# Strassen's seven products for the second layer of a fused attention and MoE kernel

## The chip, the cores and the metric

One core of one Trainium2 chip. The metric is device time in microseconds of one launch, as the median of several runs. The core has a matrix engine (PE in the profile, with PEld for its weight loads), a vector engine (DVE), an activation engine (ACT), GpSimd (POOL) and a queue engine for transfers (SP). They run beside each other and wait for each other by semaphores. PE writes its sums to PSUM banks, DVE and ACT read them from there.

## The reference

```python
# x (8, 8, 512, 64), state (8, 8, 32, 64): two small attentions per batch and head
attn_out = concat([softmax(x @ state.T / 8) @ state,
                   softmax(state @ x.T / 8) @ x], axis=2)   # (8, 8, 544, 64)
x = attn_out.transpose(0, 2, 1, 3).reshape(4352, 512)
h = x @ w_in                    # 512 -> 2048
r = maximum(h, 0)
g = s * (r * r) + b
out = g @ w_out                 # 2048 -> 512, float32
```

With the given inputs the term `b * sum(w_out)` makes up nearly the whole output: its root mean square is 0.0520, that of all the rest 0.0003 (worked out from the reference). The comparison of results therefore sees little of the product that the change is about.

## The kernel before

All matmuls are in fp16. A stage handles one batch: in sixteen steps (`f`) it computes the first layer of batch `s` (`mm1_x`, two matmuls of 512 columns into the tensor `h`), squares the result, and in between does one quarter of a 128-token block of the second layer of the batch before (`unit`, four matmuls of 512 columns into `o`). Pieces of the next batch's attention are put between the steps.

```python
def mm1_close(key, hps, ntok, f):              # after the two matmuls of a step
    ...
    nc.scalar.activation(r16[:, f % 2], hps, AF.Relu)          # ACT, 0.60 us
    if f % 2 == 1:
        gt = gpool.tile([P, 2, ntok], FP16, name=f"g_{key}_{f}", tag="g")
        nc.vector.tensor_mul(gt, r16, r16)                     # DVE, 0.69 us
        ...

def mm2_part(key, rr, f0, f1):                 # "unit": out[128 tokens] += g @ w_out
    ...
    for f in range(f0, f1):
        mm(ops, G[key, f][:, P * rr : P * rr + P], wof(f),
           start=(f == 0), stop=(f == NKF - 1))                # N = 512
    if f1 == NKF:
        ... evac(ops, ...)                     # DVE: out = s * psum + bias, then a DMA

# pieces of a stage s (cut)
at(0, lambda: att_stT(nb))
at(3, lambda: att_T(nb, [0, 1]))
at(3, lambda: att_M(nb, 0, "dve"))             # PSUM eviction on DVE, 1.2 us
...
for s in range(1, B):
    todo_s = pieces(s)
    for f in range(NKF):
        mm1_x(s, f)
        for fn in todo_s.get(f, []):
            fn()
        ...
        unit(todo.pop(0))
```

The softmax here doesn't subtract the row's maximum and nothing guards it: scores larger than these inputs give would overflow.

## Time and profile before

| | time, us | span of the profile, us | PE busy | DVE busy, us | ACT busy, us | POOL busy, us |
|---|---|---|---|---|---|---|
| before, given profile | 225.86 | 560.8 | 99% | 115.3 | 125.8 | 38.1 |
| before, profiled again in the experiments | 225.95 | 224.0 | 96% | 114.6 | 121.8 | 37.9 |

The given profile was slow: its execution lasted 560.8 us where the timed ones last 225.9. Its records show a granted clock of 1.000, so what slowed it is not shown. Lines from the page of that profile: the span, the engine totals, and two groups of instructions (line, engine, operation, what it writes and reads, shapes, count; then busy time and mean ns of one; then idle time before them and what ended it).

```profile
span 560.8 us, 3971 instructions
PE 555.9 (99%) x1628; PEld 169.0 (30%) x1628; DVE 115.3 (21%) x193; ACT 125.8 (22%) x211; POOL 38.1 (7%) x72
...
L64 PE MATMUL o<-wo,g 128*128 128x512 f16 (+1 forms) x528 | 329.7, 808 | 0.0
...
L314 DVE TENSOR_TENSOR g<-r 128x1024 f16<-128x1024 f16 x64 | 44.2, 691 | 142.0 <-ACT r L311 141.9
```

Two lines of its timeline (start, length, what, count). Thirty-two matmuls of N=512 follow each other from 528.50 to 547.55, which is 0.595 us each, and then 32 of N=256.

```profile
528.50 19.35 PE L64 MATMUL o_sr<-wo,g_sr 128*128 128x512 f16 x32
...
547.55 9.83 PE L64 MATMUL o<-wo,g 128*128 128x256 f16 x32
```

The mean of 808 ns is longer than the spacing of 595 ns: the records of neighbouring matmuls overlap.

### The profile page before, as it was taken

The numbers are of one execution on the slowest core, as the hardware profiler recorded it, in microseconds if no ns is written. First come the engines' busy times: TensorE is split into PE (matmuls) and PEld (weight loads), VectorE is DVE, ScalarE is ACT, GpSimd is POOL, SyncE is SP. The second block draws the span as 40 slices with busy tenths as digits, with TensorE's granted clock in tenths as the row PEclk, the third lists the DMA queues.
The fourth block names the chain that finished last, engine by engine and source line by source line (L and its number), as shares of the span: only waits on it lengthen the run. The fifth ranks groups of instructions, "written<-read, shape, count | busy, mean of one in ns | idle before, by whom it ended". The sixth has DMA issues, their size and how long they took to land.

```text
span 560.8 us, 3971 instructions
## 1 busy us (share of the span) xinstructions
PE 555.9 (99%) x1628; PEld 169.0 (30%) x1628; DVE 115.3 (21%) x193; ACT 125.8 (22%) x211; POOL 38.1 (7%) x72
## 2 busy tenths in 40 slices
PE   9999999999999999999999999999999999999997
PEld 3132222232233222332223223232223233334324
DVE  1442231212221212112211221112211111111101
ACT  3442122313221232113221232113221111111100
POOL 7010000100000001000010000000000000000011
DMA  9995000400060033004030120001000000000001
GB/s 202 205 132 87 1 37 9 86 19 19 1 112 20 19 75 57 19 19 76 0 56 19 39 57 20 19 19 39 11 7 19 20 19 19 19 20 19 19 19 39
DMA packets 38774, 23.69 MB, mean 42 GB/s; under 512 B 24100, under 2 KB 36644, under 8 KB 38756
## 3 DMA queue, kind: packets, MB, share of 16 engines
q0 software_dynamic: 15792, 16.72, 14.4%
q1 hardware_dynamic: 22548, 6.62, 5.8%
q8 instruction: 13, 0.21, 0.2%
q10 hardware_dynamic: 416, 0.10, 0.1%
q14 instruction: 5, 0.04, 0.0%
HBM read 17.33 MB, written 8.91 MB: 47 GB/s over the span
## 4 chain that ended last, share of the span: by engine, by line
PE 99%; DVE 0%; issue 0%
PE o L64 54%; PE h L64 27%; PE o_sr L64 3%; PE h_sr L64 3%; PE Mps L64 3%; PE warm_ps L64 2%; PE D L64 2%; PE xTps L64 1%; PE T L64 1%; PE V L64 1%; PE wsum_ps L64 0%; PE stTps L64 0%; PE bias_ps L64 0%; PE srT L64 0%; DVE M L251 0%
## 5 line engine op out<-in xcount | busy, mean ns | idle before, releaser
L64 PE MATMUL o<-wo,g 128*128 128x512 f16 (+1 forms) x528 | 329.7, 808 | 0.0
L64 PE MATMUL h<-a,M 128*128 128x512 f16 x256 | 180.2, 831 | 0.0
L311 ACT ACTIVATE r<-h 128x512 f16<-128x512 f32 x126 | 75.1, 597 | 335.9 <-PE h L64 335.9
L64 PEld LDWEIGHTS <-g 128*128 128x128 f16 x528 | 85.3, 166 | 189.5 <-issue 179.5
L64 PEld LDWEIGHTS <-M 128*128 128x128 f16 x256 | 44.4, 175 | 103.2 <-issue 102.7
L314 DVE TENSOR_TENSOR g<-r 128x1024 f16<-128x1024 f16 x64 | 44.2, 691 | 142.0 <-ACT r L311 141.9
L357 DVE SCALAR_TENSOR_TENSOR osb<-o,s_bc,bias_bc 128x512 f32<-128x512 f32 (+1 forms) x33 | 24.1, 734 | 126.5 <-PE o L64 126.5
L359 POOL DMA_DIRECT2D out_dram<-osb x31 | 16.9, 546 | 466.2 <-DVE osb L357 450.2
L256 DVE CAST M<-Mps 128x1024 f16<-128x1024 f32 x15 | 18.4, 1225 | 38.5 <-PE Mps L64 38.5
L64 PE MATMUL Mps<-wi,stT 64*32 64x512 f16 x256 | 22.8, 669 | 0.0
L64 PE MATMUL h_sr<-srdT,wi 128*128 128x256 f16 x64 | 22.6, 542 | 0.0
L64 PE MATMUL o_sr<-wo,g_sr 128*128 128x512 f16 x32 | 19.4, 836 | 0.0
L64 PEld LDWEIGHTS <-wi 128*128 128x128 f16 x64 | 11.3, 176 | 15.9 <-issue 11.9
L254 ACT CAST M<-Mps 128x1024 f16<-128x1024 f32 x13 | 13.2, 1012 | 6.4 <-PE Mps L64 6.3
L64 PEld LDWEIGHTS <-stT 64*32 64x32 f16 x384 | 5.0, 94 | 30.4 <-issue 27.9
L311 ACT ACTIVATE r_sr<-h_sr 128x256 f16<-128x256 f32 x16 | 6.1, 384 | 35.8 <-PE h_sr L64 35.8
L64 PE MATMUL warm_ps<-warm 128*128 128x512 f16 x16 | 10.0, 801 | 1.5 <-DVE warm L457 1.2
L64 PE MATMUL D<-E,bones 128*128 128x512 f16 x16 | 11.4, 813 | 0.0
L228 ACT ACTIVATE L<-D 128x1024 f32<-128x1024 f32 (+1 forms) x9 | 8.4, 929 | 11.0 <-PE D L64 11.0
L205 ACT ACTIVATE E<-T 128x512 f16<-128x512 f32 x16 | 9.4, 592 | 2.3 <-PE T L64 1.9
L64 PEld LDWEIGHTS <-g_sr 128*128 128x128 f16 x32 | 5.6, 174 | 12.8 <-issue 12.6
L229 ACT ACTIVATE R<-L 128x1024 f16<-128x1024 f32 (+1 forms) x9 | 8.7, 962 | 0.3
(58 smaller groups left out, 106.5 us busy)
## 6 DMA issues: line engine op xcount, KB each, us to landing
out_dram<-osb POOLq DMA_DIRECT2D x31, 256.0 KB, 2.5
xn<-in_x_dram POOLq DMA_DIRECT2D x7, 512.0 KB, 6.1
wi<-in_moe_w_in_dram POOLq DMA_DIRECT2D x4, 512.0 KB, 8.9
wo<-in_moe_w_out_dram POOLq DMA_DIRECT2D x4, 512.0 KB, 15.8
xf<-in_x_dram SPq DMA_DIRECT2D x2, 512.0 KB, 4.9
out_dram<-osb_sr POOLq DMA_DIRECT2D x8, 64.0 KB, 2.0
out_dram<-osb SPq DMA_DIRECT2D x2, 128.0 KB
st<-in_state_dram POOLq DMA_DIRECT2D x1, 192.0 KB, 19.8
```

What stands on the lines that cost most here:

```text
L64: return nc.tensor.matmul(out, lhsT, rhs, start=start, stop=stop, tile_position=tp, is_transpose=is_transpose, skip_group_check=True,)
L205: nc.scalar.activation(a["E"][:, g, :].rearrange("p (m t) -> p m t", m=2), T[:, :, 256 * i : 256 * i + 256], AF.Exp, scale=scale, accum_ou ...
L228: nc.scalar.activation(a["L"][:, sl], Dps, AF.Ln)
L229: nc.scalar.activation(a["R"][:, sl], a["L"][:, sl], AF.Exp, scale=-1.0)
L254: nc.scalar.copy(dst, ps)
L256: nc.vector.tensor_copy(dst, ps)
L311: nc.scalar.activation(r16[:, f % 2], hps, AF.Relu)
L314: nc.vector.tensor_mul(gt, r16, r16)
L357: nc.vector.scalar_tensor_tensor(osb, ops, s_bc, bias_bc[:, n0:n1], ALU.mult, ALU.add)
L359: eng.dma_start(dst, osb[p0:p1])
```

## The change

Intent: second-layer work on PE is by far the largest item (528 of the 1628 matmuls, nearly all of 512 columns). Strassen's method (in Winograd's form) computes a 2x2 block product with seven block products instead of eight, so the second layer of batches 1 to 6 needs 7/8 of the PE columns. The price: sums of the blocks before the products, and more complex evictions. Four sums of token blocks per batch are needed in two halves each (S1, S2 and the one that the code numbers 4 on DVE, the one numbered 3 on GpSimd), and eight differences of weight blocks once, on GpSimd. Seven products share three PSUM accumulators in two banks, `oA`, `oB` and `oC`. `q` (the first product, scaled) is taken out by ACT, GpSimd adds the bias to it twice (`qa`, `qb`), and DVE forms `u2` and `u3` from `oB` and `qa`.

Core of the diff (cut; also cut are smaller buffers that make room for the new tiles):

```diff
-            gt = gpool.tile([P, 2, ntok], FP16, ...)
-            nc.vector.tensor_mul(gt, r16, r16)
+            nc.vector.tensor_mul(gt[:, f % 4 - 1 : f % 4 + 1], r16, r16)
+    def weight_sums():
+        ...
+            out += [(t1, b12, b11), (t2, b22, t1), (t3, b22, b12), (t4, b21, t2)]
+        return [lambda o=o, a=a, c=c: nc.gpsimd.tensor_sub(o, a, c) for o, a, c in out]
+    def token_sum(b, i, j):
+        ...
+        if i == 3:
+            nc.gpsimd.tensor_sub(o, a11, a21)
+            return
+        if i == 1:
+            nc.vector.tensor_add(o, a21, a22)
+        elif i == 2:
+            nc.vector.tensor_sub(o, SQ[b, 1, j], a11)
+        else:
+            nc.vector.tensor_sub(o, a12, SQ[b, 2, j])
+        def done(p):
+            if p == 1:
+                q = keep("q")
+                nc.scalar.activation(q, acc["A"], AF.Copy, scale=s_bc)
+                nc.gpsimd.tensor_add(keep("qa"), q, blk(NH))
+                nc.gpsimd.tensor_add(keep("qb"), q, blk(0))
+            elif p == 6:
+                u = keep("u2")
+                nc.vector.scalar_tensor_tensor(u, acc["B"], s_bc, kept["qa"], ALU.mult, ALU.add)
+            ...
+        order = [(1, 0, 8), (6, 0, 4), (2, 0, 4), (6, 4, 8), (2, 4, 8), (7, 0, 8)]
+        order += [(5, 0, 8), (4, 0, 8), (3, 0, 8)]        # product, first k, last k: N = 256
         for s in range(1, B):
             ...
             for f in range(NKF):
+                if s - 1 in fast and f == 1:
+                    token_sum(s - 1, 4, 1)
                 mm1_x(s, f)
+                if s in fast:
+                    if f in (3, 7):
+                        token_sum(s, 3, f // 4)
+                    if f in (11, 12, 13):
+                        token_sum(s, (1, 2, 4)[f - 11], 0)
+                    if f == 15:
+                        token_sum(s, 1, 1)
+                        token_sum(s, 2, 1)
                 for fn in todo_s.get(f, []):
                     fn()
-                unit(todo.pop(0))
+                if s == 1 and f >= 8:
+                    sums.pop(0)()                          # the eight weight differences
+                for fn in items[f]:                        # 6 or 7 matmuls of N = 256
+                    fn()
```

More of the change, by code (lines that the diff above doesn't have):

```diff
@@ L52 @@
     apool = ctx.enter_context(tc.tile_pool(name="apool", bufs=2))
-    gpool = ctx.enter_context(tc.tile_pool(name="gpool", bufs=3 * NKF // 2))
-    rpool = ctx.enter_context(tc.tile_pool(name="rpool", bufs=6))
-    opool = ctx.enter_context(tc.tile_pool(name="opool", bufs=4))
+    gpool = ctx.enter_context(tc.tile_pool(name="gpool", bufs=2 * NKF // 4))
+    rpool = ctx.enter_context(tc.tile_pool(name="rpool", bufs=3))
+    opool = ctx.enter_context(tc.tile_pool(name="opool", bufs=3))
+    spool = ctx.enter_context(tc.tile_pool(name="spool", bufs=12))
+    upool = ctx.enter_context(tc.tile_pool(name="upool", bufs=1))
     psA = ctx.enter_context(tc.tile_pool(name="psA", bufs=2, space=bass.MemoryType.PSUM))
@@ L89 @@
     one_row = konst.tile([1, P], FP32, name="one_row")
-    stf = konst.tile([P, 2 * B, D], FP32, name="stf")
+    stf = konst.tile([P, 2 * NPE, D], FP32, name="stf")
     st16 = konst.tile([P, 2 * B, 2, D], FP16, name="st16")
     gate = konst.tile([1, 1], FP16, name="gate")
-    xf = konst.tile([P, NG, NQ, SCH * D], FP32, name="xf")
+    xf = apool.tile([P, NG, NQ, SCH * D], FP32, name="xf", tag="M")
     s_bc = konst.tile([P, 1], FP32, name="s_bc")
@@ L103, with new_xn @@
     wo = [wpool.tile([P, NKF // 4, DM], FP16, name=f"wo_{q}") for q in range(4)]
-    xn = [xpool.tile([P, H, SCH, D], FP16, name=f"xn_{b}") for b in range(B)]
+    wd = [[wpool.tile([P, 4, DM // 2], FP16, name=f"wd{i}_{j}") for j in range(2)] for i in range(4)]
+    xn = {}
+    def new_xn(b):
+        xn[b] = xpool.tile([P, H, SCH, D], FP16, name=f"xn_{b}", tag="xn", bufs=5)
+    new_xn(0)
     def load_x(b):
+        new_xn(b)
         nc.gpsimd.dma_start(
@@ L201, in att_T @@
         if gs[0] == 0:
-            a["E"] = apool.tile([P, NG, S], FP16, name=f"E_{b}", tag="E", bufs=4)
+            a["E"] = apool.tile([P, NG, S], FP16, name=f"E_{b}", tag="E", bufs=3)
             a["rs"] = apool.tile([P, NG], FP32, name=f"rs_{b}", tag="rs", bufs=4)
@@ L295 @@
     G = {}
+    G4 = {}
     R2 = {}
@@ L311, in mm1_close @@
             nc.scalar.activation(r16[:, f % 2], hps, AF.Relu)
+        if f % 4 == 0:
+            G4[key, f // 4] = gpool.tile([P, 4, ntok], FP16, name=f"g_{key}_{f}", tag="g")
+        gt = G4[key, f // 4]
+        G[key, f] = gt[:, f % 4]
         if f % 2 == 1:
-            gt = gpool.tile([P, 2, ntok], FP16, name=f"g_{key}_{f}", tag="g")
-            nc.vector.tensor_mul(gt, r16, r16)
-            G[key, f - 1] = gt[:, 0]
-            G[key, f] = gt[:, 1]
+            nc.vector.tensor_mul(gt[:, f % 4 - 1 : f % 4 + 1], r16, r16)
     def mm1_k(b, f, g, hps):
@@ L386, in mm2_part @@
                 late.pop()()
+    NH = DM // 2
+    TH = S // 2
+    def weight_sums():
+        out = []
+        for j in range(2):
+            b11, b12 = wo[j][:, :, 0:NH], wo[j][:, :, NH:DM]
+            b21, b22 = wo[2 + j][:, :, 0:NH], wo[2 + j][:, :, NH:DM]
+            t1, t2, t3, t4 = (wd[i][j] for i in range(4))
+            out += [(t1, b12, b11), (t2, b22, t1), (t3, b22, b12), (t4, b21, t2)]
+        return [lambda o=o, a=a, c=c: nc.gpsimd.tensor_sub(o, a, c) for o, a, c in out]
+    SQ = {}
@@ new lines, in token_sum @@
+    def token_sum(b, i, j):
+        SQ[b, i, j] = spool.tile([P, 4, TH], FP16, name=f"s{i}_{b}_{j}", tag="s")
+        o = SQ[b, i, j]
+        a11, a21 = G4[b, j][:, :, 0:TH], G4[b, j][:, :, TH:S]
+        if i == 3:
+            nc.gpsimd.tensor_sub(o, a11, a21)
+            return
+        a12, a22 = G4[b, 2 + j][:, :, 0:TH], G4[b, 2 + j][:, :, TH:S]
+        if i == 1:
[4 more added lines that the diff above has]
+            nc.vector.tensor_sub(o, a12, SQ[b, 2, j])
@@ new lines, in fast_items, with lhs, rhs, keep @@
+    def fast_items(b):
+        acc = {}
+        kept = {}
+        def lhs(p, k, i):
+            c = P * i
+            if p == 1:
+                return G[b, k][:, c : c + P]
+            if p == 2:
+                return G[b, 8 + k][:, c : c + P]
+            if p == 4:
+                return G[b, 8 + k][:, TH + c : TH + c + P]
+            si = {3: 4, 5: 1, 6: 2, 7: 3}[p]
+            return SQ[b, si, k // 4][:, k % 4, c : c + P]
+        def rhs(p, k):
+            if p == 1:
+                return wof(k)[:, 0:NH]
+            if p == 2:
+                return wof(8 + k)[:, 0:NH]
+            if p == 3:
+                return wof(8 + k)[:, NH:DM]
+            ti = {4: 3, 5: 0, 6: 1, 7: 2}[p]
+            return wd[ti][k // 4][:, k % 4, :]
+        def keep(name):
+            kept[name] = upool.tile([P, 2, NH], FP32, name=f"{name}_{b}", tag=name)
+            return kept[name]
+        def put(bank, add, j, n0):
+            osb = opool.tile([P, 2, NH], FP32, name=f"osb_{b}_{j}_{n0}", tag="osb")
+            nc.vector.scalar_tensor_tensor(osb, acc[bank], s_bc, add, ALU.mult, ALU.add)
+            dst = out_BSn[b, 0:S].rearrange("(q ci cj) n -> cj q ci n", ci=2, cj=2)
+            nc.gpsimd.dma_start(dst[j][:, :, n0 : n0 + NH], osb)
+        def blk(n0):
+            return bias_bc[:, n0 : n0 + NH].unsqueeze(1).broadcast_to([P, 2, NH])
+        def done(p):
+            if p == 1:
+                q = keep("q")
[5 more added lines that the diff above has]
+                nc.vector.scalar_tensor_tensor(u, acc["B"], s_bc, kept["qa"], ALU.mult, ALU.add)
+            elif p == 2:
+                put("A", blk(0), 0, 0)
+            elif p == 7:
+                u = keep("u3")
+                nc.vector.scalar_tensor_tensor(u, acc["B"], s_bc, kept["qa"], ALU.mult, ALU.add)
+            elif p == 5:
+                put("C", kept["u3"], 1, NH)
+            elif p == 4:
+                put("B", kept["qb"], 1, 0)
+            else:
+                put("C", kept["u2"], 0, NH)
+        def item(p, k, i):
+            bank = {1: "A", 2: "A", 6: "B", 7: "B", 4: "B", 5: "C", 3: "C"}[p]
+            fresh = p in (1, 6, 5)
+            if fresh and k == 0 and i == 0:
+                acc[bank] = psO.tile([P, 2, NH], FP32, tag="o", name=f"o{bank}_{b}")
+            mm(
+                acc[bank][:, i, :],
+                lhs(p, k, i),
+                rhs(p, k),
+                start=(fresh and k == 0 and i == 0),
+                stop=(k == 7),
+            )
+            if k == 7 and i == 1:
+                done(p)
+        order = [(1, 0, 8), (6, 0, 4), (2, 0, 4), (6, 4, 8), (2, 4, 8), (7, 0, 8)]
+        order += [(5, 0, 8), (4, 0, 8), (3, 0, 8)]
+        return [
+            lambda p=p, k=k, i=i: item(p, k, i)
+            for p, k0, k1 in order
+            for k in range(k0, k1)
+            for i in range(2)
+        ]
@@ L438 @@
     units = []
-    for b in range(B):
+    for b in (0, B - 1):
         for i in range(NKF):
@@ L573, in pieces @@
             if s + 3 < B:
-                at(9, lambda: load_x(s + 3))
+                at(13 if s == 2 else 9, lambda: load_x(s + 3))
             if nb < B:
@@ L597, in pieces @@
             return out
+        sums = weight_sums()
+        fast = range(1, B - 1)
+        coming = {}
         for s in range(1, B):
             todo_s = pieces(s)
+            if s in fast:
+                coming[s] = fast_items(s)
+            first = coming[s][:16] if s in fast else []
+            if s == 1:
+                items = [[] for _ in range(NKF)]
+                for f in [*range(4), *range(5, 13)]:
+                    items[f] = [lambda u=todo.pop(0): unit(u)]
+                items[13], items[14], items[15] = first[0:4], first[4:10], first[10:16]
+            else:
+                flat = coming[s - 1][16:] + first
+                n = -(-len(flat) // NKF)
+                items = [flat[n * f : n * f + n] for f in range(NKF)]
             for f in range(NKF):
+                if s - 1 in fast and f == 1:
+                    token_sum(s - 1, 4, 1)
                 mm1_x(s, f)
+                if s in fast:
+                    if f in (3, 7):
[5 more added lines that the diff above has]
+                        token_sum(s, 2, 1)
                 for fn in todo_s.get(f, []):
                     fn()
-                if s == 1 and f == 4:
-                    continue
-                unit(todo.pop(0))
+                if s == 1 and f >= 8:
+                    sums.pop(0)()
+                for fn in items[f]:
+                    fn()
+                if s == last_b and f in (14, 15):
+                    unit(todo.pop(0))
         for f in range(4, NKF):
```

## The prediction

> **What bounds the kernel now.** TensorE. The chain of waits is 99% PE, and PE is busy 99% of the span (engine totals); DVE is at 115.3 us, ACT 125.8, POOL 38.1. But the profiled execution lasted 560.8 us against 225.86 us timed, and its matmuls are slow: 32 second-layer matmuls of N=512 took 19.05 us from first to next (timeline, 528.50 to 547.55), 0.595 us each. So "99% PE" is not proven for the timed runs, where DVE, ACT and GpSimd keep their durations and have 2.4 times less time to hide in. Counted from the code, about 909 matmuls of 512 columns (or their equivalent) follow the start. The Trainium skill ("TensorE: Matmul & The Clock Gate", Back-to-back issue gap) gives N/2.4+2.5 ns, 216 ns each: about 196 us. Start (first h matmul at 16.6 us in the trace, about 14 with a fast PE) and tail bring it to about 215 us; the other 10 us are small stalls or visible weight loads. PE-bound, but not by 99%.
>
> **What is removed.** Per batch the second layer goes from 64 matmuls of 512 columns to 112 of 256: 7/8 of the columns. Six batches save 96 x 256 = 24576 columns, an estimated 10.2 us at 2.4 columns/ns. The number of weight loads rises by 288. N=256 streams well in the trace: the last 32 took 9.8 us, 0.30 us each, half of N=512, so loads are mostly hidden; in the timed clock 2.5 to 10 ns each may show, costing 1 to 3 us. Gross gain 7.5 to 9.5 us.
>
> **What is added.**
> - DVE: per batch six fp16 sums of 128x1024 (0.69 us each, as the g multiplies) and two more 128x512 PSUM evictions (0.73): +5.6 us on about 12.8, of a batch of about 23 us: 80% busy.
> - ACT: one 0.6 us eviction per batch.
> - GpSimd: per batch two 128x1024 differences, two 128x512 fp32 adds; once, eight weight differences of 128x1024. Trace copies on POOL run about 1 ns per element (128x768: 0.83 us). For two inputs the skill ("GPSIMD Engine Reference", 3.1) measures 2.6 cycles per element; my estimate is 2.25 us each, 18 us for eight. No trace shows one yet.
>
> **What lies on the critical path.** The eight weight differences start after the second token difference of batch 1, about step 10 of stage 1, and stand in front of the first q additions in GpSimd's order. The first P6 (second half) needs the sixth weight difference about 11 us after that start, and P7 needs u2, hence qa, after about 14.5 us; they are ready after about 15 and 22 us. So PE should wait once, 4 to 8 us, early in stage 2. In each batch u2 follows an M eviction (1.2 us) on DVE with about 1.5 us of slack: 0.3 to 0.5 us of stall, about 2 us in all. Other banks have 16 matmuls of slack.
>
> Sum: 225.9 - 8.5 + 5 + 2 = about 224 us; 8 in 10 between 217.5 and 230. Chances: faster by over 2% 0.32, within 2% 0.56, slower 0.12.
>
> **What would show it.** PE matmuls 288 more, PE busy less in proportion; GpSimd weight differences near 2.2 us; PE waits on T sums or u2 near the start of stage 2 (smaller or absent if the profile again has a slow PE); DVE busy about 150 us.
>
> **What would make it wrong.** GpSimd differences of 1.3 us or less: no stall, about 218. DVE and GpSimd blocking each other, or weight loads exposed at N=256: 230 or more.

## More of the kernel before

The order of instructions on PE, SP and GpSimd is that of the program. On DVE and ACT it is chosen when the kernel is built.

The line PEclk gives, for 40 equal slices of the span, the granted clock of PE in tenths.

```profile
span 224.0 us, 3971 instructions
PE 215.8 (96%) x1628; PEld 98.5 (44%) x1628; DVE 114.6 (51%) x193; ACT 121.8 (54%) x211; POOL 37.9 (17%) x72
...
PEclk9999999999999999999999999999999999999999
...
L64 PE MATMUL o<-wo,g 128*128 128x512 f16 (+1 forms) x528 | 131.1, 373 | 0.9 <-DVE osb L357 0.9
L314 DVE TENSOR_TENSOR g<-r 128x1024 f16<-128x1024 f16 x64 | 44.6, 698 | 41.7 <-ACT r L311 41.5
```

PE is busy 96% of the time, its clock is never reduced, and DVE's multiplies take 0.70 us each. The matmuls are 0.216 us apart (N=512). In a regular stage of 23.46 us PE makes no wait that matters.

## The result, and the profile after

The changed kernel takes 241.65 us (median of four runs, 241.26 to 241.94) against 225.87 us: ratio 1.0695, interval 1.0676 to 1.0714, slower by 7%. A ratio is the mean time of one kernel's fast runs over that of the other's fast runs of the same rounds, so it is not quite the ratio of the medians. The profiled execution is fast. Lines of its page, to be set beside those of the fast profile of before, and, from its list of all groups, half of the weight differences:

```profile
span 240.1 us, 4655 instructions
PE 211.6 (88%) x1916; PEld 127.3 (53%) x1916; DVE 168.9 (70%) x241; ACT 124.7 (52%) x217; POOL 103.5 (43%) x104
...
PEclk9999999999575899999999999999999999999999
...
L327 DVE TENSOR_TENSOR g<-r 128x1024 f16<-128x1024 f16 x64 | 56.7, 893 | 21.3 <-ACT r L321 21.2
L419 POOL TENSOR_TENSOR s<-g 128x1024 f16<-128x1024 f16 x12 | 25.4, 2118 | 35.0 <-DVE g L327 34.9
```

```profile
L410 POOL TENSOR_TENSOR wd<-wo,wd 128x1024 f16<-128x1024 f16 x4 | 8.9, 2235 | 0.1
```

Three things are to be seen. PE's busy time did fall, by 4.2 us, although its matmuls rose from 1628 to 1916. The same DVE multiply (g<-r) that took 698 ns on average now takes 893 ns, though it is the same instruction with the same shape. And PEclk has a dip that it did not have before.

The stages show where the time went. A stage is here the time from the first `h` matmul of one batch to that of the next, worked out from the trace; stage 7 includes the tail. Stage 0 has none of the new products.

| us | start | stage 0 | stage 1 | stage 2 | stages 3 to 6, each | stage 7 and tail |
|---|---|---|---|---|---|---|
| before (fast profile) | 11.77 | 18.28 | 25.71 | 24.31 | 23.46 | 50.14 |
| after | 11.10 | 18.91 | 31.72 | 35.09 | 23.30 | 50.12 |

Stages 1 and 2 lost 16.8 us together. And each regular stage won only 0.16 us, where seven products instead of eight should win 1.58 us (64 matmuls at 0.2158 us against 112 at 0.1092, the spacings of N=512 and N=256 in this trace).

**Stages 1 and 2.** The view of waits (engine, line, what it waited for; total us, times, longest) names DVE each time that PE stood still for long:

```profile
PE oB L66 <- DVE s L425: 6.7, 1, 6.7
PE h L66 <- DVE a L239: 5.9, 2, 5.2
...
PE oB L66 <- DVE u L475: 5.1, 5, 1.2
```

The timeline of PE there, with the wait in brackets at the end of a line:

```profile
55.70 0.82 PE L66 MATMUL oA<-wo,g 128*128 128x256 f16 x6
61.73 1.03 PE L66 MATMUL h<-a,M 128*128 128x512 f16 x2 [5.21 <-DVE a L239]
...
62.77 1.70 PE L66 MATMUL oB<-wd,s 128*128 128x256 f16 x7
64.26 1.06 PE L66 MATMUL h<-a,M 128*128 128x512 f16 x2
...
66.59 0.38 PE L66 MATMUL oA<-wo,g 128*128 128x256 f16 x2
73.69 1.25 PE L66 MATMUL oB<-wd,s 128*128 128x256 f16 x5 [6.72 <-DVE s L425]
```

PE stood still for 5.2 and 6.7 us. What DVE did in that time:

```profile
53.62 1.95 DVE L423 TENSOR_TENSOR s<-g,g 128x1024 f16<-128x1024 f16 x1
55.60 2.50 DVE L425 TENSOR_TENSOR s<-s,g 128x1024 f16<-128x1024 f16 x1
...
58.69 2.98 DVE L239 TENSOR_TENSOR a<-E,R 128x1024 f16<-128x1024 f16 x1
61.59 9.31 DVE L327 TENSOR_TENSOR g<-r 128x1024 f16<-128x1024 f16 x1
70.82 0.68 DVE L427 TENSOR_TENSOR s<-g,s 128x1024 f16<-128x1024 f16 x1
```

And GpSimd:

```profile
52.44 2.58 POOL L410 TENSOR_TENSOR wd<-wo,wo 128x1024 f16<-128x1024 f16 x1
54.98 2.57 POOL L410 TENSOR_TENSOR wd<-wo,wd 128x1024 f16<-128x1024 f16 x1
...
58.98 2.13 POOL L410 TENSOR_TENSOR wd<-wo 128x1024 f16<-128x1024 f16 x1
...
61.65 2.13 POOL L410 TENSOR_TENSOR wd<-wo,wd 128x1024 f16<-128x1024 f16 x1
63.73 2.12 POOL L410 TENSOR_TENSOR wd<-wo,wo 128x1024 f16<-128x1024 f16 x1
65.80 2.12 POOL L410 TENSOR_TENSOR wd<-wo,wd 128x1024 f16<-128x1024 f16 x1
67.88 1.25 POOL L471 TENSOR_TENSOR qa<-q,bias_bc 128x512 f32<-128x512 f32 x1
69.09 1.25 POOL L472 TENSOR_TENSOR qb<-q,bias_bc 128x512 f32<-128x512 f32 x1
```

The first wait ended with `a` (58.69 to 61.67), which DVE did beside the weight difference of 58.98 to 61.11: 2.98 us, where the same multiply takes 0.68 us in a regular stage (131.91 in this trace). Then one DVE multiply that takes 0.68 us elsewhere "took" 9.31 us, from 61.59 to 70.90. In that time GpSimd ran three weight differences and the two q additions back to back, from 61.65 to 70.34. DVE finished half a microsecond after the last of them. DVE's long bar is thus not work but a wait inside the instruction, and it counts as busy time on the page. After it DVE still had to do the sums that PE waited for (`s`, line 425), and PE went on at 73.69.

The clock is part of the price. After the first wait seven matmuls of N=256 take 1.49 us (62.77 to 64.26), 0.213 us each; in a regular stage seven of them take 0.76 us, 0.109 each. PE ran at half rate until about 65.7 and again from 73.7 to about 79.3. Summing, over both stretches, what each matmul's spacing exceeds that of the regular stages gives about 4.3 us lost on top of the waits.

**Regular stages.** One wait per stage is left, of this form (timeline of stage 4, DVE and PE):

```profile
126.08 1.21 DVE L265 CAST M<-Mps 128x1024 f16<-128x1024 f32 x1
127.21 0.74 DVE L475 SCALAR_TENSOR_TENSOR u<-oB,s_bc,qa 128x512 f32<-128x512 f32 x1
128.00 0.49 PE L66 MATMUL oB<-wd,s 128*128 128x256 f16 x3 [1.20 <-DVE u L475]
```

The seventh product accumulates into the bank that `u2` is read from, so it must wait for `u2`. DVE does `u2` only after an eviction of M of 1.2 us. PE's spacing shows 1.36 us lost at that place in every regular stage (the trace names 1.20 of it). That is nearly the whole gain.

### The profile page after: what moved, and what is told of

It reads as the page before. It is cut to its first block, busy times and chain, and to the rows that moved or that the text cites. A ratio compares the mean times of both kernels' runs of the same rounds, so it can differ in the third digit from the quotient of the medians.

```text
span 240.1 us, 4655 instructions
## 1 busy us (share of the span) xinstructions
PE 211.6 (88%) x1916; PEld 127.3 (53%) x1916; DVE 168.9 (70%) x241; ACT 124.7 (52%) x217; POOL 103.5 (43%) x104
## 4 chain that ended last, share of the span: by engine, by line
PE 56%; DVE 28%; DMA 7%; issue 4%; ACT 2%; POOL 1%; SPq 0%; DVEq 0%
PE h L66 14%; DVE g L327 10%; PE oB L66 10%; PE o L66 9%; PE oC L66 8%; DMA xn<-in_x_dram 5%; DVE s L425 4%; DVE s L427 4%; PE h_sr L66 3%; PE o_sr L66 3%; DVE s L423 3%; PE Mps L66 3%; PE oA L66 3%; DMA xf<-in_x_dram 2%; DVE u L475 2%
## 5 line engine op out<-in xcount | busy, mean ns | idle before, releaser
L66 PE MATMUL h<-a,M 128*128 128x512 f16 x256 | 76.9, 387 | 6.4 <-DVE a L239 5.9
L66 PEld LDWEIGHTS <-g 128*128 128x128 f16 x432 | 41.4, 99 | 24.6 <-issue 5.6
L66 PEld LDWEIGHTS <-s 128*128 128x128 f16 x384 | 36.5, 100 | 29.9 <-issue 10.2
L419 POOL TENSOR_TENSOR s<-g 128x1024 f16<-128x1024 f16 x12 | 25.4, 2118 | 35.0 <-DVE g L327 34.9
L66 PE MATMUL oB<-wd,s 128*128 128x256 f16 x192 | 29.7, 285 | 11.8 <-DVE s L425 6.7
L66 PEld LDWEIGHTS <-M 128*128 128x128 f16 x256 | 24.9, 99 | 16.3 <-DVE a L239 5.5
L66 PE MATMUL o<-wo,g 128*128 128x512 f16 (+1 forms) x144 | 32.3, 356 | 0.9 <-DVE osb L368 0.9
L66 PE MATMUL oA<-wo,g 128*128 128x256 f16 x192 | 28.6, 278 | 0.3 <-DVE osb L368 0.3
L265 DVE CAST M<-Mps 128x1024 f16<-128x1024 f32 x15 | 18.3, 1218 | 1.6 <-PE Mps L66 1.6
L425 DVE TENSOR_TENSOR s<-s,g 128x1024 f16<-128x1024 f16 x12 | 14.5, 1208 | 0.2
L66 PE MATMUL oC<-wd,s 128*128 128x256 f16 x96 | 14.3, 273 | 0.0
```

The costliest lines, as they stand in the source:

```text
L66: return nc.tensor.matmul(out, lhsT, rhs, start=start, stop=stop, tile_position=tp, is_transpose=is_transpose, skip_group_check=True,)
L265: nc.vector.tensor_copy(dst, ps)
L419: nc.gpsimd.tensor_sub(o, a11, a21)
L425: nc.vector.tensor_sub(o, SQ[b, 1, j], a11)
```

## The experiments

Two theories stood at this point. A: the loss in stages 1 and 2 comes from GpSimd's run of operations with two inputs, which shuts DVE out. B: every stage loses its gain to DVE's queue and to GpSimd's smaller operations. Rivals: the products themselves are slow, since each matmul of N=256 has a weight load of its own (C), or DVE simply has too much work.

### x0_before: the kernel before, profiled again

No edit.

> The kernel before, unchanged, to get a profile in the same fast state as that of the changed kernel. Every theory: timed about 225.9 us; if the profile is of the fast state, span about 224 us, N=512 matmuls about 0.216 us apart, a stage of one batch about 24 us, PE waiting little in stages 1 and 2. If PE turns out to wait a lot in the kernel before, the gross gain of the change was not 9.5 us.

Measured: 225.95 us, span 224.0 us (a single run). Its lines are shown above. Stages of 23.46 us instead of "about 24". The gross gain that the prediction counted on was there to be had.

### e5_halves: the kernel before with matmuls of N=256

```diff
-            mm(ops, G[key, f][:, P * rr : P * rr + P], wof(f),
-               start=(f == 0), stop=(f == NKF - 1))
+            for n0 in (0, DM // 2):
+                mm(ops[:, n0 : n0 + DM // 2], G[key, f][:, P * rr : P * rr + P],
+                   wof(f)[:, n0 : n0 + DM // 2],
+                   start=(f == 0 and n0 == 0), stop=(f == NKF - 1))
```

> The kernel before, with every second-layer matmul of N=512 split into two of N=256 with the same weights, each with its own weight load: about 496 more loads and matmuls, same columns. If loads are hidden (the changed kernel's trace shows N=256 matmuls 0.109 us apart), plus 1 to 2 us, about 227.3 us. Theory C (N=256 exposes loads): 10 ns or more each, plus 5 us or more, 231 us or more.

Measured: 227.62 us, ratio 1.0079 (1.0037 to 1.0122). The page counts 528 more matmuls and loads (the state rows were split as well), so one costs about 3.4 ns (1.8 us by the ratio over 528; the regular stages, 23.62 us with 64 more each, give 2.5 ns). Theory C is out as the cause of the loss: 288 more loads cost about 1 us.

### e1_wsum_dve: the weight differences on DVE

```diff
-        return [lambda o=o, a=a, c=c: nc.gpsimd.tensor_sub(o, a, c) for o, a, c in out]
+        return [lambda o=o, a=a, c=c: nc.vector.tensor_sub(o, a, c) for o, a, c in out]
```

> The changed kernel with the eight weight differences on DVE instead of GpSimd (one word). Theory A (the loss is the once-only block of GpSimd two-input operations in stages 1 and 2, during which a DVE multiply took 9.31 us): about 15 to 20 us come back, 222 to 226 us, PE waits of 5.2 and 6.7 us near 56 and 67 us gone. Theory B (the loss is in every batch: q additions and token difference on GpSimd against DVE): under 6 us come back, 236 us or more. Theory C (weight loads at N=256 cost PE time): nothing comes back beyond the two waits.

Measured: 237.01 us, ratio 1.0473. By the number alone this is theory B's case (236 or more), but the trace shows another reason. The experiment was flawed: with the work on DVE, whose order is chosen when the kernel is built, the first difference was put into stage 0, in front of what PE needed, and waited for its weights to arrive:

```profile
14.61 0.69 DVE L327 TENSOR_TENSOR g<-r 128x1024 f16<-128x1024 f16 x1
22.88 0.69 DVE L410 TENSOR_TENSOR wd<-wo 128x1024 f16<-128x1024 f16 x1 [7.58 <-DMA wo<-in_moe_w_out_dram]
```

Stage 0 took 29.06 us instead of 18.91. Stages 1 and 2, however, took 24.87 and 26.13 us, as theory A expected. The run supports A but can't price it.

### e3_both_dve: weight differences and q additions on DVE

```diff
-                nc.gpsimd.tensor_add(keep("qa"), q, blk(NH))
-                nc.gpsimd.tensor_add(keep("qb"), q, blk(0))
+                nc.vector.tensor_add(keep("qa"), q, blk(NH))
+                nc.vector.tensor_add(keep("qb"), q, blk(0))
```

> As e1, and the two q additions of each batch on DVE too; GpSimd keeps only the token difference a11-a21. Theory A alone: no faster than e1, DVE has 8 us more work. With theory B as a second term: the PE wait for u2 of about 1.2 us per batch goes, 5 to 7 us better than e1, about 218 us. Rival: DVE, now near 20 us of 23 per batch, becomes the limit and e3 is as slow as e1 or slower.

Measured: 233.05 us, ratio 1.0308, with the same flaw in stage 0 (29.79 us). Regular stages fell from 23.30 to 22.92 us: 0.4 us each, not 1.2. Stage 2 fell from 26.13 us in e1 to 24.63. PE's loss before the seventh product shrank only from 1.36 to 1.05 us. So GpSimd's q additions are a small part of that wait, and theory B's first form, that they cause it, falls.

### e6_wsum_dve_late: weight differences on DVE, held back to stage 1

```diff
+        def one(o, a, c):
+            nc.gpsimd.memset(o[0:1, 0, 0:1], 0.0)      # one element, keeps the order
+            nc.vector.tensor_sub(o, a, c)
-        return [lambda o=o, a=a, c=c: nc.gpsimd.tensor_sub(o, a, c) for o, a, c in out]
+        return [lambda o=o, a=a, c=c: one(o, a, c) for o, a, c in out]
```

> As e1 (weight differences on DVE, GpSimd keeps everything else), but each waits for a one-element GpSimd memset that comes at its old place in stage 1, so that DVE does not meet them in stage 0 and wait 8 us for the weights' transfer as in e1. Theory A (once-only block of DVE by the run of GpSimd two-input operations): stages 1 and 2 shrink from 31.7 and 35.1 us to about 25 and 25, 225.5 us in all, later stages unchanged at 23.3 us. If the GpSimd block was not the cause of the long stages, DVE's extra 5.5 us make them no shorter and the time stays over 235 us.

Measured: 231.72 us, ratio 1.0231 (1.0169 to 1.0293, so slower, but by 2% or not stays unclear). Its runs spread from 229.38 us, at full clock, to 232.18, with a dip of the clock. Stages 1 and 2: 26.32 and 29.96 us. Ten microseconds came back, but not sixteen. In the trace four of the eight differences were released only at about 55 to 56 us, since the memsets stood behind an output transfer in GpSimd's order, and they came before the sums that stage 2 needs; two of them took 1.75 us each beside the q additions. PE lost 4.3 us there. So where the differences stand matters as well as which engine does them.

### e7_no_wsum: no weight differences at all (wrong on purpose)

```diff
-            ti = {4: 3, 5: 0, 6: 1, 7: 2}[p]
-            return wd[ti][k // 4][:, k % 4, :]
+            return wof(k)[:, 0:NH]
...
-                if s == 1 and f >= 8:
-                    sums.pop(0)()
```

> The changed kernel with the eight weight differences left out; the products read plain weights instead, so the result is wrong on purpose; same matmuls, same other work. It bounds what the differences cost wherever they stand. Theory A: stages 1 and 2 near 25 and 24.5 us, about 224.5 us, not more than 1 to 2 us below e6. Rival (the token sums and q additions alone already stretch stages 1 and 2): 232 us or more.

Measured: 227.00 us, ratio 1.0043; stages 1 and 2: 25.76 and 26.13 us. The eight differences, where the change placed them, cost 241.65 - 227.00 = 14.7 us, against 5 us in the prediction. What is left is 1 us over the kernel before, although the products save PE time: the view of waits of e7 names six waits on `u2`, 6.0 us together, and one of 1.3 us early in stage 2, on a token sum that DVE did beside the q additions (1.72 and 1.55 us for two sums instead of 0.69). Its output is wrong, which doesn't matter for the time.

### e8_before_sub and e9_before_memset: the block by itself, in the kernel before

```diff
                 for fn in todo_s.get(f, []):
                     fn()
+                if s == 1 and f >= 8:
+                    nc.gpsimd.tensor_sub(idle, wo[0][:, :, 0:256], wo[2][:, :, 0:256])   # e8
+                    nc.gpsimd.memset(xf, 0.0)                                           # e9
```

(One line each; `idle` is a new tile, `xf` one that is no longer used. An unused part of another tile was cut to make room.)

> The kernel before, plus eight GpSimd differences of two 128x1024 fp16 inputs into an idle tile, at the same place (stage 1, steps 8 to 15); nothing reads them, the result is right. If GpSimd operations with two SBUF inputs shut DVE's two-input multiplies out, DVE multiplies of 0.69 us stretch to 2 us and more, a2 comes late and PE waits: plus 4 to 12 us, 230 to 238 us. If GpSimd mattered only by what waits for its results, nothing changes: 226 us.

> As e8, but eight GpSimd memsets of 128x2048 fp32 (about 1.7 to 2 us each, no input) instead of the differences. If it is the read side that GpSimd and DVE contend for, DVE multiplies stay at 0.69 us and the time at 226 us. If any GpSimd work of that length holds DVE up, it is as slow as e8.

Measured: e8 232.50 us, ratio 1.0283 (1.0247 to 1.0320); e9 225.65 us, ratio 0.9983 (0.9951 to 1.0016). Nobody reads what either computes. DVE and GpSimd in e8:

```profile
43.68 5.08 DVE L315 TENSOR_TENSOR g<-r 128x1024 f16<-128x1024 f16 x2
48.68 1.21 DVE L257 CAST M<-Mps 128x1024 f16<-128x1024 f32 x1
...
52.83 3.60 DVE L231 TENSOR_TENSOR a<-E,R 128x1024 f16<-128x1024 f16 x1 [0.22 <-ACT R L230]
56.35 5.27 DVE L315 TENSOR_TENSOR g<-r 128x1024 f16<-128x1024 f16 x2
```

```profile
43.56 7.18 POOL L607 TENSOR_TENSOR idle<-wo,wo 128x1024 f16<-128x1024 f16 x3
...
56.41 7.19 POOL L607 TENSOR_TENSOR idle<-wo,wo 128x1024 f16<-128x1024 f16 x3
```

And in e9, in the same stretch:

```profile
52.85 0.69 DVE L230 TENSOR_TENSOR a<-E,R 128x1024 f16<-128x1024 f16 x1 [0.59 <-ACT R L229]
53.46 0.68 DVE L314 TENSOR_TENSOR g<-r 128x1024 f16<-128x1024 f16 x1
```

```profile
42.94 5.53 POOL L606 MEMSET xf<- 128x2048 f32 x3
...
52.63 1.84 POOL L606 MEMSET xf<- 128x2048 f32 x1
...
54.92 5.56 POOL L606 MEMSET xf<- 128x2048 f32 x3
```

Beside three GpSimd differences in a row two multiplies of DVE last 5.08 us from start to end instead of 1.4; the eviction of M, which reads PSUM, keeps its 1.21 us although the third difference still runs (until 50.74). Beside memsets of 1.84 us each the multiplies take 0.68 or 0.69: the two shown lie beside the single memset of 52.63, two more (43.70 and 46.30) beside the first three. So it is not GpSimd's activity as such; what differs is that the differences read SBUF and the memsets do not. (A GpSimd operation that reads one input was not tried.) The Trainium skill says so ("SBUF — State Buffer", Who interferes with whom): a DVE instruction with two SBUF inputs contends with a GpSimd instruction that reads SBUF, not with one that only writes it. The two runs agree, and price it here at 6.7 us, a stretch at half clock included (58.9 to 65.6 us in e8). This is clean evidence for theory A, since nothing of Strassen's method is in these kernels.

### e10_m0_later: one piece moved by one step

```diff
-                at(3, lambda: att_M(nb, 0, "dve"))
+                at(4, lambda: att_M(nb, 0, "dve"))
```

> The changed kernel with one piece moved: the first M block of the next batch (a PSUM eviction of 1.2 us on DVE) is issued at step 4 of a stage instead of step 3, so that DVE meets u2 before it. If the wait of 1.36 us in each later stage (between the second product and the seventh, on u2) is this queue order on DVE, stages 3 to 6 fall from 23.3 us to about 22.0 and the whole by 5 to 6 us, to about 236; stages 1 and 2 stay long. If the wait comes from qa (GpSimd) or from PE's own rate, they stay at 23.3.

Measured: 236.56 us, ratio 1.0459 (the unmoved kernel: 1.0695). Regular stages: 22.18 us instead of 23.30; stages 1 and 2 stay at 31.75 and 34.27 us. No PE wait on `u2` is left there. The wait was the order of two instructions in DVE's queue, as expected.

### e11_early_m0, e12_early_m0_q, e13_early_m0_all: towards a version that wins

e11 is e10 with the weight differences on DVE, released at step 4 of stage 1 and issued one per step from 4 to 11:

```diff
+        for o, _, _ in out:
+            nc.gpsimd.memset(o[0:1, 0, 0:1], 0.0)
+        return [lambda o=o, a=a, c=c: nc.vector.tensor_sub(o, a, c) for o, a, c in out]
...
-        sums = weight_sums()
+        sums = []
-                if s == 1 and f >= 8:
+                if s == 1 and f == 4:
+                    sums = weight_sums()
+                if s == 1 and 4 <= f < 12:
                     sums.pop(0)()
```

e12 adds the two q additions on DVE (the edit of e3), e13 also the token difference:

```diff
         if i == 3:
-            nc.gpsimd.tensor_sub(o, a11, a21)
+            nc.vector.tensor_sub(o, a11, a21)
```

> e10, and the weight differences on DVE, released at step 4 of stage 1 and issued one per step from 4 to 11 (in e6 they stood at steps 8 to 15 and four of them were released only at 55 us, in front of the sums that stage 2 needs). Stages 1 and 2 about 26 and 23.5 us, later ones 22.0: about 218 us, the first version faster than the kernel before by over 2%. If stage 2 stays near 26 us or more, the differences were not the last obstacle there.

> e11 with the two q additions of a batch on DVE instead of GpSimd. If their block of DVE still costs PE anything once u2 comes in time: 0.3 us a stage, about 2 us better than e11. If not: the same within 0.5 us, or worse by up to 2 us because qa now stands in front of the sum that product 6 needs.

> e12 with the token difference on DVE too: no GpSimd arithmetic left in the second layer. DVE then has about 20.5 us of work in a stage of 22. If DVE's queue is the next limit, slower than e12 by 1 to 4 us; if the block by GpSimd mattered more, faster.

| | time, us | ratio to before | stage 1 | stage 2 | stages 3 to 6 | stage 7 and tail |
|---|---|---|---|---|---|---|
| e11 | 223.57 | 0.9874 | 27.83 | 25.25 | 22.18 | 50.12 |
| e12 | 221.45 | 0.9783 | 27.80 | 23.81 | 22.10 | 49.66 |
| e13 | 219.06 | 0.9674 (0.9645 to 0.9703) | 25.35 | 23.81 | 22.10 | 49.69 |

e11 missed its 218: stages 1 and 2 were still 1.8 us longer than expected each. e12 took back 1.4 us in stage 2, where in e11 the q additions held up the sum before the sixth product. For e13 the expectation was loss if DVE's queue was the next limit, and gain if the block mattered more: it gained 2.4 us, all in stage 1, where in e11 and e12 one multiply had taken 3.05 and 3.02 us beside a token difference on GpSimd. In e11 PE waits 0.97 us on `stT` just after it and 1.75 us on an M eviction later in the stage; e13 has neither wait. (In e7 the multiply takes 2.89 us too, but without weight differences on DVE only the first of these waits follows, 0.81 us.) The page of e13:

```profile
span 217.1 us, 4651 instructions
PE 207.6 (96%) x1916; PEld 126.1 (58%) x1916; DVE 159.4 (73%) x273; ACT 123.8 (57%) x217; POOL 41.4 (19%) x80
```

DVE does all the arithmetic that GpSimd did, and is busy 159.4 us; in the changed kernel it was "busy" 168.9 us while doing less. So the rival that DVE has too much work falls as well. The version with no GpSimd arithmetic beats the kernel before by 3.3%. Its arithmetic is that of the changed kernel, operation by operation; only engines and places differ, and eight one-element memsets are added.

## Why the prediction was wrong

- *"PE-bound, but not by 99%"*, and the slow given profile: right. The fast profile shows PE busy 96%, and 0.216 us per matmul of N=512, which is what the skill's formula gave. (The skill means this formula for single matmuls and gives a smaller figure for streams, see the last section; the trace sides with the formula.)
- *"Gross gain 7.5 to 9.5 us"*: right. e10's regular stages gain 1.28 us and e13's 1.36 us over the kernel before, against 1.58 by the count of columns; six such stages would be 7.7 to 8.2 us. e5 puts the loads at 3.4 ns each, and e13 wins 7.3 us in all (226.35 - 219.06, the medians of its rounds).
- *"my estimate is 2.25 us each, 18 us for eight"*: right, 2.12 to 2.58 us each in the trace, 18.3 in all. The skill ("GPSIMD Engine Reference", Elementwise — side-by-side cycle accounting) gives about 2.6 cycles per element; 2.12 us for 1024 elements at the 1.2 GHz it states are 2.5.
- *"PE should wait once, 4 to 8 us, early in stage 2"*: this is the step that failed. The prediction followed data only: which result does PE need, and when is GpSimd done with it. The sixth weight difference was ready at 63.8 us and PE asked for it after 66.6, so it was not what PE waited for. The same GpSimd operations shut DVE out, so that multiplies, a2 and sums of DVE which do not depend on GpSimd at all came late, and PE waited twice, 5.2 and 6.7 us. That the second wait stood where the prediction expected one, before the second half of the sixth product, and was 4 to 8 us long, is luck: it was a wait for a DVE sum. Term of the sum: 5 us predicted, 14.7 us measured (changed kernel minus e7). About 4.3 us of that is the half clock after the waits, which the sum did not contain. The prediction named "DVE and GpSimd blocking each other" among what would make it wrong, but gave it no term in the sum, though the page that states it could be read beforehand and DVE's multiplies all have two SBUF inputs.
- *"u2 follows an M eviction (1.2 us) on DVE ... 0.3 to 0.5 us of stall, about 2 us in all"*: the mechanism was right, the size was not. It was 1.36 us in each of the regular stages, and e10 got back 5.1 us by moving that eviction. Why the slack of 1.5 us was not there is only in part shown: in the trace DVE was still behind when the eviction came, by sums that ran beside the q additions (1.56 and 1.64 us instead of 0.69), but e3, where they take 0.68, still lost 1.05 us. So about 0.3 us is the q additions' part, and the rest is that `u2` stood behind the eviction at all.
- *"DVE busy about 150 us"*: 168.9, of which e13's total for more work, 159.4, shows that 9.5 us or more was waiting inside instructions.

Put together, with the waits that e7 shows beside the differences: 225.9 - 8.5 + 14.7 + 6.0 (six waits on `u2`) + 1.3 (one on a sum in stage 2) is 239.4, near the 241.65 measured; the last 2 us are not accounted for. Left open: why DVE got in between single GpSimd operations in some stretches (two sums of 1.95 and 2.50 us between 53 and 58 us) but was passed over five times in a row in the longest one, where its multiply's recorded start (61.59) is even before that of the first of the five (61.65; GpSimd's times are rough).

## What to carry to other kernels

Moving elementwise work to an idle GpSimd was not free for DVE here: where both read SBUF and the DVE operation had two SBUF inputs, DVE stood still for GpSimd's slower operation (5.08 us for two multiplies in e8), and whatever waited for DVE stood still as well, related or not. A DVE instruction that took longer than its twin of the same shape was waiting in these traces, though the page counts it as busy; look at what GpSimd does in that time. And a saving of one and a half microseconds in a stage was lost to a single instruction that stood in the wrong place of DVE's queue (e10), so look for that before giving up the idea.

## What the Trainium skill lacked or had wrong

- "SBUF — State Buffer", Who interferes with whom: it states the block for one instruction. Neither it nor another page says that DVE can be passed over by several GpSimd instructions in a row: here by five, and a multiply of 0.69 us lasted 9.31 us. Nor that such a wait is shown as the instruction's own busy time.
- "TensorE: Matmul & The Clock Gate", Back-to-back issue gap: for streams of load and matmul it gives a sustained 131 ns per matmul at N=512. Here each matmul has its own load and they are 216 ns apart (N=512) and 109 ns (N=256), which is its formula for single matmuls.
- The same page, Why this matters for your kernels: it asks for no idle gaps of PE over about 3 us. In e8 the rate halved inside the second of two waits, of 0.71 and 1.96 us (ending at 56.49 and 59.16), neither near 3: the granted clock is 1.00 from 57.2 to 58.8 us and 0.50 from 58.9 to 65.6 (two N=512 matmuls then took 0.85 us, 62.51 to 63.36, against 0.43 in the regular stages). So that row alone is too lenient here; elsewhere the page does tell of short, frequent idling that makes the clock swing.
- "GPSIMD Engine Reference": its two-input figure is for fp32 alone. Here fp16 with 1024 elements takes 2.11 to 2.13 us where DVE does not hold it up, against an estimate of 2.2 us by that figure (2.6 cycles at 1.2 GHz), so the narrower type brings hardly any gain.
